# Two transformer layers in fp32: first norm tile by tile, another order of the first weights and products, and transposes tied behind the w1 matmuls

## Chip, core and metric

The kernel runs on one core of one Trainium2 chip. A core has TensorE (PE, matmuls), VectorE (DVE), ScalarE (ACT), GpSimd (POOL) and SyncE (SP), each with its own instruction queue that is worked in order; DMAs are issued from SP, ACT and POOL. PE writes into PSUM banks, the others work on SBUF. The metric is the device time of one execution in microseconds.

## The reference

Two blocks, attention (A) and an MLP with the mish activation (B), run twice in turn on x of 2048 rows by 512, with shared weights for both layers, all float32:

```python
def _A_ref(x, wqkv, wo):        # H = 32 heads of Dh = 16
    qkv = (x @ wqkv).reshape(B, S, 3, H, Dh) ...
    scores = jnp.einsum("bhqd,bhkd->bhqk", q, k) * (Dh ** -0.5)
    p = _softmax(scores, axis=-1)
    o = jnp.einsum("bhqk,bhkd->bhqd", p, v)
    return o.transpose(...).reshape(B, S, D) @ wo
def _B_ref(x, w1, b1, w2):      # F = 1792
    h = jnp.einsum("bsd,df->bsf", x, w1) + b1
    act = h * jnp.tanh(stable_softplus(h))
    return jnp.einsum("bsf,fd->bsd", act, w2)
x = x + _A_ref(_layernorm(x), wqkv, wo)
x = x + _B_ref(_layernorm(x), w1, b1, w2)
x = x + _A_ref(_layernorm(x), wqkv, wo)
x = x + _B_ref(_layernorm(x), w1, b1, w2)
```

## The kernel before

The 2048 rows are held as four chunks c of 512 rows, each chunk as four tiles of 128 rows. A float32 operand of a matmul is split into a rounded high part and the low part that is left; `mm3` (L174) makes of one product three matmuls per step k of 128 (high by high, high by low, low by high). High parts are written by ACT, low parts by DVE or POOL (`split_psum` L170, the inner `split` of `split_load` L132).

**The first stage (qkv of layer 0).** Chunk c is normed by `norm_parts` (L181): per tile `bn_stats` and `bn_aggr` on DVE (stq, mvq), variance plus epsilon on DVE (veq, L188), its power of -1/2 on POOL (rsq, L189), the scaling on DVE (xnq, L209), then transposes on PE through the bank pair tpq (L222), and the high and low part, thq on ACT and tlq on DVE, two tiles (a half of 256 columns) at a time. `norm_parts` is a generator; its parts are called from the loop of products in `qkv` at the places that the tables `within` (L729 on) give as (number of the product, step k). The products (m, c) follow the list `order`: m 0 to 3 are q, 4 to 7 are k, two m to one weight block of 256 columns. Products one to five are (0,0), (4,0), (1,0), (5,0) and (0,1), so the first two need chunk 0 and the weights sqkv0 and sqkv2, and the fifth is the first to need chunk 1. Each product's result is split into pt (ACT, then DVE) and stored by a DMA on ACT's queue (scr). Before the data are there, PE runs matmuls on zeros (`warm_up`, WARM).

**Values and maxima.** After q and k come the value products of chunks 0 to 2 (`v_parts`, parts of three or more matmuls, va), with the first row maxima of the scores mixed in by `some_max`: two pairs of matmuls into a bank pair each (pm, tag mx, two bank pairs), each reduced by DVE (mxv, L331). Then the attention loop starts with scores (sp, ss) and the value products of chunk 3 (vp), which use the bank pairs of tag mx.

**The MLP.** For the pairs (c, f), f from 0 to 13, `hid` makes h from the w1 block (three matmuls for each of four k), a chain on ACT, DVE and POOL makes the activation's high and low part, and `outp`, two f later, adds its w2 products into mo. Between them stand the last attention projections (wo) in c = 0, and the norms of later chunks: `spread` hangs the parts of a norm behind `hid` of given (c, f). Weights w1 and w2 are loaded by SP in the order of the program, each when a buffer of the pool blk comes free. Outside of the stages where PE's order is written out by hand (`att.pe`), the build orders the instructions of each engine by itself from program order and data, and may pull a transpose of a norm ahead of the matmuls that stand before it in the program.

Of the kernel before, what the change touches and what calls it, by code (L numbers as in the profile page):

```python
# [10 lines left out]
F32R = mybir.dt.float32r  # L11
BF16 = mybir.dt.bfloat16
AF = mybir.ActivationFunctionType
ALU = mybir.AluOpType
# [4 lines left out]
P = 128  # L19
S, D, H, DH, F = 2048, 512, 32, 16, 1792  # L20
NCH = 4
# [21 lines left out]
FILL = 12  # L43
KEEP = 2
PREP = 7
WARM = (4, 3)
GSTEPS = NCH * NKT
STEPS = NG * GSTEPS
HEADS = STEPS * HG
# [19 lines left out]
def kernel(ctx: ExitStack, tc: tile.TileContext, x, wqkv, wo, w1, b1, w2, out):  # L69
# [24 lines left out]
    def b8(shape, dt, name):  # L94
        return blk.tile(shape, dt, tag="blk", name=name)
# [21 lines left out]
    def behind(ins):  # L117
        return tc.keep_in_program_order(ins)
# [7 lines left out]
    def split_load(key, src, a, b, later, raw=None, low=nc.gpsimd):  # L126
        t = b8([P, 2, a, b], F32R, "s" + key)
        if raw is None:
            raw = tmp.tile([P, a, b], F32, tag="raw", name="r" + key, bufs=3)
        behind(nc.sync.dma_start(raw, src))  # L130

        def split():  # L132
            behind(nc.scalar.activation(t[:, 0], raw, AF.Copy))
            behind(low.tensor_tensor(t[:, 1], raw, t[:, 0].bitcast(F32), op=ALU.subtract))
            unkept.append((key, t))

        later.append(split)
        return t

    def split_keep(hooks, at, key, src, a, b):  # L140
# [40 lines left out]
    def norm_parts(src, nm, got, key, tag, fine=False, pin=lambda ins: ins, pe=lambda ins: ins, halves=False):  # L181
        st = tmp.tile([P, NCH, 6], F32, tag="st", name=f"st{nm}")
        mv = tmp.tile([P, NCH, 2], F32, tag="mv", name=f"mv{nm}")
        ve = tmp.tile([P, NCH], F32, tag="ve", name=f"ve{nm}")
        rs = tmp.tile([P, NCH], F32, tag="rs", name=f"rs{nm}")

        def rstd(t, n):
            pin(nc.vector.tensor_scalar(ve[:, t : t + n], mv[:, t : t + n, 1], EPS, None, op0=ALU.add))  # L188
            nc.gpsimd.tensor_tensor(rs[:, t : t + n], ve[:, t : t + n], mhalf[:, t : t + n], op=ALU.pow)  # L189

        for t in range(NCH):
            pin(nc.vector.bn_stats(st[:, t], src[:, t]))
            pin(nc.vector.bn_aggr(mv[:, t], st[:, t]))
            if fine:
                rstd(t, 1)
        if not fine:
            rstd(0, NCH)
        yield
        th = b8([P, KT, CW], F32R, f"th{nm}")
        tl = b8([P, KT, CW], F32R, f"tl{nm}")  # L200
        got[key] = (th, tl)

        def scaled(t, tag):
            if tag == "raw":
                xn = tmp.tile([P, 2, 512], F32, tag=tag, name=f"xn{nm}{t}", bufs=3)[:, 0]
            else:
                xn = t512(tag, f"xn{nm}{t}")
            pin(
                nc.vector.tensor_scalar(  # L209
                    xn, src[:, t], mv[:, t, 0:1], rs[:, t : t + 1], op0=ALU.subtract, op1=ALU.mult  # L210
                )
            )
            return xn

        if tag == "mx":
            xns = [scaled(t, ("f", "ah")[t // 2]) for t in range(NCH)]
            yield
            for u in range(NCH // 2):
                tp = ps.tile([P, 2, 512], F32, tag=tag, name=f"tp{nm}{u}")
                for e in range(2):  # L220
                    for k in range(KT):
                        pe(nc.tensor.transpose(tp[:, e, ts(k, P)], xns[2 * u + e][:, ts(k, P)], ident))  # L222
                two = ts(u, 2 * P)
                split_psum(
                    th[:, :, two].rearrange("p k (t n) -> p k t n", n=P),
                    tl[:, :, two].rearrange("p k (t n) -> p k t n", n=P),
                    tp.rearrange("p t (k n) -> p k t n", n=P),
                    pin,
                )
                yield  # L230
            return
        for t in range(NCH):
            xn = scaled(t, "raw" if tag == "acc" else "f")
            if halves:
                yield
            tp = pbank(tag, f"tp{nm}{t}")
            for k in range(KT):
                pe(nc.tensor.transpose(tp[:, ts(k, P)], xn[:, ts(k, P)], ident))
            split_psum(th[:, :, ts(t, P)], tl[:, :, ts(t, P)], tp.rearrange("p (k n) -> p k n", k=KT), pin)
            yield  # L240

    def spread(hooks, at, src, nm, got, key):
        parts = norm_parts(src, nm, got, key, "acc")
        for c, f in at:
            hooks.setdefault((c, f), []).append(lambda: next(parts, None))

# [211 lines left out]
    def load_qkv(l, wts, which, later, low=nc.gpsimd):  # L458
        raw = None
        for j in which:  # L460
            key = f"qkv{j}"
            if l:
                wts[j] = ready(key, l, True)
            elif j < 4:
                wts[j] = split_load(key, *cols(wqkv, j), later, low=low)
            else:
                if raw is None:
                    raw = b8([P, 2, 2, D], F32, "rawv")
                wts[j] = split_load(key, *rows2(wqkv[:, 2 * D : 3 * D], j - 4), later, raw[:, j - 4])
# [4 lines left out]
    def qkv(l, att, wts, tt, order, within, due):  # L474
        scr = att.scr
        ahead = [0]

        def some_max():
            if ahead[0] < AHEAD + PRE:
                for n in range(2):  # L480
                    att.max_mm(ahead[0], n)
                ahead[0] += 1

        done = 0
        spare = []
        parts = iter(())
        for n, (m, c) in enumerate(order):
            for fn in within.get((n, 0), []):
                fn()
            w = wts[m // 2]  # L490
            if n % 2:
                if not spare:
                    two = b8([P, 2, 2, CW], F32R, f"pt{l}{m}{c}")
                    spare += [two[:, 0], two[:, 1]]
                pt = spare.pop(0)
            else:
                pt = tmp.tile([P, 2, CW], F32R, tag="raw", name=f"pt{l}{m}{c}", bufs=3)
            th, tl = tt[c]
            acc = pbank("s", f"qk{l}{c}{m}")
            for k in range(KT):  # L500
                for fn in within.get((n, k), []) if k else []:
                    fn()
                mm3(
                    acc,
                    [(w[:, 0, k, ts(m % 2, P)], w[:, 1, k, ts(m % 2, P)], th[:, k], tl[:, k])],
                    first=k == 0,
                    last=k == KT - 1,
                    pe=att.pe,
                )
            split_psum(pt[:, 0], pt[:, 1], acc)  # L510
            nc.scalar.dma_start(
                scr[m][:, :, ts(c, CW)].bitcast(F32).rearrange("a p n -> p a n"), pt.bitcast(F32)
            )
            for fn in due.get((m, c), []):
                fn()
            for _ in range(2):
                next(parts, None)
            if m in (0, 4):
                done += 1
                if done == 2 * NCH:  # L520
                    parts = att.prep_qk(0)
                    for _ in range(2 * PREP):
                        next(parts)
            elif done == 2 * NCH and m in MAX_M:
                some_max()
        i = 0
        for c in range(NCH - 1):
            for _ in v_parts(l, c, wts, tt, att, False):
                i += 1
                if i % 3 == 0:  # L530
                    some_max()

    def v_parts(l, c, wts, tt, att, paired):
# [88 lines left out]
    def mlp(l, x2s, w1t, w2t, tts, dst, hooks):  # L622
        acts, obs = {}, {}

        def hid(c, f):
# [3 lines left out]
            mm3(  # L629
                acc,  # L630
                [(w[:, 0, k, ts(f % 2, P)], w[:, 1, k, ts(f % 2, P)], th[:, k, :], tl[:, k, :]) for k in range(KT)],
            )
            nm = f"{l}{c}{f}"
            hb, e, r = t512("f", "hb" + nm), t512("he", "he" + nm), t512("hr", "hr" + nm)
# [63 lines left out]
            keep(*unkept.pop(0))  # L698

    xc = [load_x(0)]  # L700
    load_qkv(0, wts, (0, 2), splits, nc.vector)
    xc += [load_x(c) for c in range(1, NCH)]
    nc.sync.dma_start(b1t, b1.rearrange("(f p) -> p f", p=P))
    att = attention(0)
    att.chained = True
    norms = [norm_parts(xc[c], f"q0{c}", tt, c, "mx", c == 0, behind, att.pe) for c in range(NCH)]
    warm = b8([P, CW], F32, "warm")
    nc.vector.memset(warm, 0.0)

# [3 lines left out]
            att.pe(nc.tensor.matmul(acc, warm[:, 0:P], warm, start=True, stop=True))  # L713

    warm_up(0, WARM[0])
    for i in range(4):
        next(norms[0])
        if i > 1:
            splits.pop(0)()
    warm_up(1, WARM[1])  # L720
    for l in range(2):
        due, within = {}, {}
        if l == 0:
# [2 lines left out]
            due[4, 2] = [lambda: load_qkv(0, wts, (4, 5), later)]  # L726
            due[0, 3] = [lambda: split_all(splits)]
            due[5, 2] = [lambda: split_all(later)]
            for c, (n0, n1, n2) in enumerate(((0, 0, 2), (2, 3, 5), (4, 6, 7)), 1):  # L729
                for at in ((n0, 0), (n1, 0), (n2, 1), (n2, 3)):  # L730
                    within.setdefault(at, []).append(lambda c=c: next(norms[c]))
        else:
            order = [(0, 0), (0, 1), (4, 0), (4, 1), (1, 0), (0, 2), (4, 2), (1, 1), (1, 2), (5, 0), (5, 1), (0, 3), (4, 3)]
# [126 lines left out]
```

## Time and profile before

| | |
|---|---|
| runs | 3551.27, 3558.86, 3556.11 us; median 3556.11 |
| profiled execution | 3554.46 us, span 3552.7 us |
| granted TensorE clock, mean | 0.999 |
| qkv and values, layer 0 | 0 to 168 us |
| attention loop, layer 0 | 168 to 1424 us |
| projections and MLP, layer 0 | 1424 to 1790 us |
| qkv and values, layer 1 | 1790 to 1934 us |
| attention loop, layer 1 | 1934 to 3189 us |
| projections and MLP, layer 1 | 3189 to 3553 us |

A row of the timeline has the start in us from the span's start, the us from its first start to its last end, the engine (ACTq and SPq are issues of DMAs; PEld are weight loads), the source line, the operation, what it writes <- reads, the shape, the number of instructions merged into the row, and in brackets the idle time of the engine before it with what ended it. Busy times of matmuls are modelled and overlap: the step from start to start tells PE's pace. A row of a table of windows has, after the window and its length, the busy us (and instructions) of PE, PEld, DVE, ACT and POOL, then the granted clock, the share of the DMA engines and GB/s.

### The profile page before, as it was taken

The numbers are of one execution on the slowest core, as the hardware profiler recorded it, in microseconds if no ns is written. First come the engines' busy times: TensorE is split into PE (matmuls) and PEld (weight loads), VectorE is DVE, ScalarE is ACT, GpSimd is POOL, SyncE is SP. The second block draws the span as 40 slices with busy tenths as digits, with TensorE's granted clock in tenths as the row PEclk, the third lists the DMA queues.
The fourth block names the chain that finished last, engine by engine and source line by source line (L and its number), as shares of the span: only waits on it lengthen the run. The fifth ranks groups of instructions, "written<-read, shape, count | busy, mean of one in ns | idle before, by whom it ended". The sixth has DMA issues, their size and how long they took to land.

```text
span 3552.7 us, 69170 instructions
## 1 busy us (share of the span) xinstructions
PE 3531.6 (99%) x28718; PEld 1938.4 (55%) x28718; DVE 2963.1 (83%) x3039; ACT 2520.7 (71%) x3401; POOL 521.6 (15%) x571
## 2 busy tenths in 40 slices
PE   9999999999999999999999999999999999999999
PEld 7644444444444444778876444444444444447887
DVE  5789999999999994756646999999999999947555
ACT  3188888888888888344522888888888888874444
POOL 2100100000000002444410000000000000024443
PEclk9999999999999999999999999999999999999999
DMA  7641312213132124510164211112111121245100
GB/s 250 218 99 47 83 44 76 59 52 71 44 80 46 45 80 70 159 60 13 59 221 140 53 37 39 38 29 44 32 35 38 41 35 41 68 78 161 50 13 24
DMA packets 139430, 255.11 MB, mean 72 GB/s; under 512 B 29348, under 2 KB 73316, under 8 KB 125292
## 3 DMA queue, kind: packets, MB, share of 16 engines
q1 hardware_dynamic: 112196, 174.04, 19.6%
q10 hardware_dynamic: 19176, 43.06, 3.4%
q0 software_dynamic: 7744, 33.60, 3.3%
q8 instruction: 225, 3.69, 0.5%
q14 instruction: 89, 0.73, 0.1%
HBM read 149.43 MB, written 100.14 MB: 70 GB/s over the span
## 4 chain that ended last, share of the span: by engine, by line
PE 95%; DMA 2%; DVE 1%; issue 1%; ACT 1%; POOL 1%; ACTq 0%; SPq 0%; DVEq 0%; POOLq 0%
PE pv L401 30%; PE pm L327 17%; PE ss L385 13%; PE sp L375 10%; PE mo L179 3%; PE mo L177 3%; PE mo L178 3%; PE h L179 3%; PE h L177 3%; PE h L178 3%; PE qk L177 1%; PE qk L178 1%; PE qk L179 1%; PE va L177 1%; PE wo L177 1%
## 5 line engine op out<-in xcount | busy, mean ns | idle before, releaser
L331 DVE TENSOR_REDUCE mxv<-pm 128x2 f32<-128x1024 f32 x2048 | 2385.6, 1218 | 135.5 <-PE pm L327 85.1
L376 ACT ACTIVATE p<-sp 128x1024 f32<-128x1024 f32 x1366 | 1395.9, 1022 | 19.3 <-PE sp L375 15.0
L401 PE MATMUL pv<-p,va 128*32 128x256 f32 (+2 forms) x16032 | 1166.9, 392 | 0.1
L327 PE MATMUL pm<-ks,qs 48*128 48x512 f32 x4096 | 1096.5, 446 | 0.3
L386 ACT ACTIVATE p<-ss 128x512 f32<-128x512 f32 x1364 | 814.5, 597 | 348.6 <-PE ss L385 263.1
L375 PE MATMUL sp<-qs,ks 50*128 50x512 f32 x2732 | 726.2, 447 | 0.3
L401 PEld LDWEIGHTS pv<-p,va 128*32 128x32 f32 x16032 | 367.7, 108 | 499.2 <-issue 421.5
L327 PEld LDWEIGHTS pm<-ks,qs 48*128 48x128 f32 x4096 | 450.0, 184 | 345.7 <-issue 210.0
L385 PE MATMUL ss<-qs,ks 50*128 50x512 f32 x1364 | 611.0, 448 | 0.0
L385 PEld LDWEIGHTS ss<-qs,ks 50*128 50x128 f32 x1364 | 252.0, 185 | 329.5 <-ACT p L386 222.8
L375 PEld LDWEIGHTS sp<-qs,ks 50*128 50x128 f32 x2732 | 261.3, 183 | 200.3 <-ACT p L376 119.1
L346 POOL CAST np<-nt 128x32 fp32r<-128x32 f32 x64 | 13.3, 208 | 2214.0 <-DVE nt L344 2214.0
L642 POOL TENSOR_TENSOR hb<-hb,he 128x512 f32<-128x512 f32 x110 | 149.2, 1356 | 190.3 <-DVE he L638 186.2
L645 POOL TENSOR_TENSOR hb<-hb,hr 128x512 f32<-128x512 f32 x110 | 150.5, 1368 | 139.5 <-DVE ah L644 134.7
L644 DVE TENSOR_TENSOR ah<-hb,hr 128x512 fp32r<-128x512 f32 x112 | 77.1, 689 | 111.5 <-ACT hr L640 67.2
L639 ACT ACTIVATE hr<-he 128x512 f32<-128x512 f32 x112 | 70.8, 632 | 125.0 <-DVE he L638 82.2
L635 ACT ACTIVATE hb<-h,b1t 128x512 f32<-128x512 f32 x112 | 77.0, 687 | 111.8 <-PE h L179 102.9
L637 ACT ACTIVATE he<-he 128x512 f32<-128x512 f32 x112 | 70.8, 632 | 103.0 <-DVE he L636 97.6
L171 ACT ACTIVATE pt<-qk 128x512 fp32r<-128x512 f32 x64 | 37.8, 597 | 148.4 <-PE qk L179 109.9
L636 DVE TENSOR_SCALAR he<-hb 128x512 f32<-128x512 f32 x112 | 70.8, 632 | 70.3 <-ACT hb L635 60.0
L646 DVE TENSOR_TENSOR al<-hb,ah 128x512 fp32r<-128x512 f32 x112 | 88.3, 789 | 32.5 <-POOL hb L645 32.3
L638 DVE SCALAR_TENSOR_TENSOR he<-he 128x512 f32<-128x512 f32 x112 | 79.7, 712 | 28.4 <-ACT he L637 27.5
(232 smaller groups left out, 3245.0 us busy)
## 6 DMA issues: line engine op xcount, KB each, us to landing
scr<-pt ACTq DMA_DIRECT2D x64, 512.0 KB
qs<-scr SPq DMA_DIRECT2D x174, 128.0 KB
ks<-scr SPq DMA_DIRECT2D x174, 128.0 KB
vscr<-v SPq DMA_DIRECT2D x32, 512.0 KB
va<-vscr SPq DMA_DIRECT2D x64, 256.0 KB
oscr<-ot SPq DMA_DIRECT2D x64, 256.0 KB
ww<-sw POOLq DMA_DIRECT2D x14, 1024.0 KB, 4.8
num<-oscr SPq DMA_DIRECT2D x64, 128.0 KB
```

Source lines behind the costliest of these rows:

```text
L177: pe(nc.tensor.matmul(acc, ah, bh, start=first and i == 0, stop=False))
L178: pe(nc.tensor.matmul(acc, ah, bl, start=False, stop=False))
L179: pe(nc.tensor.matmul(acc, al, bh, start=False, stop=last and i == n - 1))
L327: nc.tensor.matmul(pm[:, e], qs[u][rows, q0 : q0 + P], ks[u][rows, ts(n, 512)], start=True, stop=True)
L331: nc.vector.tensor_reduce(self.mxs[b][:, 2 * u : 2 * u + 2, qt, n], pm, axis=AX.X, op=ALU.max)
L375: self.pe(nc.tensor.matmul(sp[:, e], k, q, start=True, stop=True))
L376: nc.scalar.activation(self.pts[-1][:, 0:n], sp[:, 0:n], AF.Exp, scale=SCALE)
L385: self.pe(nc.tensor.matmul(sp, k, q, start=True, stop=True))
L386: nc.scalar.activation(self.pts[i // 3][:, 2], sp, AF.Exp, scale=SCALE)
L401: nc.tensor.matmul(self.accs[b][ts(h, VW), cols], self.va[b // NCH][:, kt, h, :], self.pts[j][:, e, cols], start=kt == 0 and q0 == 0, stop ...
L642: mul.tensor_tensor(hb, hb, e, op=ALU.mult)
L645: mul.tensor_tensor(hb, hb, r, op=ALU.mult)
```

## The change

- WARM is (4, 1, 1) in place of (4, 3); one matmul on zeros stands between the two halves' transposes of chunk 0, one behind them.
- `split` becomes two steps, `high` and `lowpart`, called apart. The first weight's high part is called before the first thq. The second weight's low part moves from DVE to POOL.
- The addition of epsilon moves from DVE to POOL, in all norms. The norms of the first stage are fine: each tile has its own addition and power, and each tile's scaling follows on DVE behind the next tile's statistics.
- The first two products of layer 0 are ordered by parts: high by high, low weight by high, high by low (the second with its last two exchanged), four matmuls each.
- The places of chunk 1 to 3's norm parts among the products move.
- `some_max` is called after value parts 1, 4, 7, ... in place of 3, 6, 9, ... in both layers.
- In both MLPs, transposes of a norm are tied to stand behind the last matmul of the `hid` that was issued before them.

```diff
-WARM = (4, 3)
+WARM = (4, 1, 1)
...
-        def split():
+        def high():
             behind(nc.scalar.activation(t[:, 0], raw, AF.Copy))
+
+        def lowpart():
             behind(low.tensor_tensor(t[:, 1], raw, t[:, 0].bitcast(F32), op=ALU.subtract))
             unkept.append((key, t))
-        later.append(split)
+        later += [high, lowpart]
...
         def rstd(t, n):
-            pin(nc.vector.tensor_scalar(ve[:, t : t + n], mv[:, t : t + n, 1], EPS, None, op0=ALU.add))
+            nc.gpsimd.tensor_scalar(ve[:, t : t + n], mv[:, t : t + n, 1], EPS, None, op0=ALU.add)
...
+        def next_scaled():
+            xns.append(scaled(len(xns), ("f", "ah")[len(xns) // 2]))
+
+        for t in range(NCH):
+            pin(nc.vector.bn_stats(st[:, t], src[:, t]))
+            pin(nc.vector.bn_aggr(mv[:, t], st[:, t]))
+            if fine:
+                rstd(t, 1)
+                if t and tag == "mx":
+                    next_scaled()
...
         if tag == "mx":
-            xns = [scaled(t, ("f", "ah")[t // 2]) for t in range(NCH)]
+            while len(xns) < NCH:
+                next_scaled()
...
+    hidden = []
+
+    def behind_hidden(ins):
+        tc.add_manual_dep(ins.ins, hidden[-1].ins.name, ..., reason="issue order")
...
-        parts = norm_parts(src, nm, got, key, "acc")
+        parts = norm_parts(src, nm, got, key, "acc", pe=behind_hidden)
...
-            for k in range(KT):
+            if l == 0 and n < 2:
+                for i, (part, t) in enumerate(((0, th), (0, tl), (1, th)) if n else ((0, th), (1, th), (0, tl))):
+                    for k in range(KT):
+                        start, stop = i == k == 0, i == 2 and k == KT - 1
+                        att.pe(nc.tensor.matmul(acc, w[:, part, k, ts(m % 2, P)], t[:, k], start=start, stop=stop))
+            for k in range(KT if l or n > 1 else 0):
...
-                if i % 3 == 0:
+                if i % 3 == 1:
                     some_max()
...
+                pe=lambda ins: hidden.__setitem__(slice(None), [ins]),
...
-    load_qkv(0, wts, (0, 2), splits, nc.vector)
+    load_qkv(0, wts, (0,), splits, nc.vector)
+    load_qkv(0, wts, (2,), splits)
...
-    norms = [norm_parts(xc[c], f"q0{c}", tt, c, "mx", c == 0, behind, att.pe) for c in range(NCH)]
+    norms = [norm_parts(xc[c], f"q0{c}", tt, c, "mx", True, behind, att.pe) for c in range(NCH)]
...
-    for i in range(4):
-        next(norms[0])
-        if i > 1:
-            splits.pop(0)()
+    next(norms[0])
+    splits.pop(0)()
+    next(norms[0])
+    next(norms[0])
     warm_up(1, WARM[1])
+    splits.pop(0)()
+    next(norms[0])
+    warm_up(2, WARM[2])
+    split_all(splits)
...
-            for c, (n0, n1, n2) in enumerate(((0, 0, 2), (2, 3, 5), (4, 6, 7)), 1):
-                for at in ((n0, 0), (n1, 0), (n2, 1), (n2, 3)):
+            for c, spots in enumerate((((0, 0), (0, 0), (2, 2), (3, 1)), ((2, 0), (2, 0), (5, 1), (5, 3)), ((4, 0), (4, 0), (7, 1), (7, 3))), 1):
+                for at in spots:
```

More of the change, by code (lines that the diff above doesn't have):

```diff
@@ L187, in rstd @@
         def rstd(t, n):
-            pin(nc.vector.tensor_scalar(ve[:, t : t + n], mv[:, t : t + n, 1], EPS, None, op0=ALU.add))
+            nc.gpsimd.tensor_scalar(ve[:, t : t + n], mv[:, t : t + n, 1], EPS, None, op0=ALU.add)
             nc.gpsimd.tensor_tensor(rs[:, t : t + n], ve[:, t : t + n], mhalf[:, t : t + n], op=ALU.pow)
[L191 to L201, printed above, removed]
+        xns = []
         def scaled(t, tag):
@@ L213, in scaled @@
             return xn
+        def next_scaled():
[7 more added lines that the diff above has]
+                    next_scaled()
+        if not fine:
+            rstd(0, NCH)
+        yield
+        th = b8([P, KT, CW], F32R, f"th{nm}")
+        tl = b8([P, KT, CW], F32R, f"tl{nm}")
+        got[key] = (th, tl)
         if tag == "mx":
-            xns = [scaled(t, ("f", "ah")[t // 2]) for t in range(NCH)]
+            while len(xns) < NCH:
+                next_scaled()
             yield
@@ L240, in norm_parts @@
             yield
+    hidden = []
+    def behind_hidden(ins):
+        tc.add_manual_dep(
+            ins.ins,
+            hidden[-1].ins.name,
+            mybir.DependencyInfo(mybir.DependencyClass.NoSync, mybir.DependencyReason.DATA),
+            reason="issue order",
+        )
     def spread(hooks, at, src, nm, got, key):
-        parts = norm_parts(src, nm, got, key, "acc")
+        parts = norm_parts(src, nm, got, key, "acc", pe=behind_hidden)
         for c, f in at:
```

## The prediction

> **What bounds the kernel now.** I read the page's first part, then the idle time of TensorE by what ended it, then the timeline of the first 31 us, of the places where a stage ends, and of the stop in the second half of the MLP.
>
> ```profile
> span 3552.7 us, 69170 instructions
> PE 3531.6 (99%) x28718; PEld 1938.4 (55%) x28718; DVE 2963.1 (83%) x3039; ACT 2520.7 (71%) x3401; POOL 521.6 (15%) x571
> ...
> PE tpq L222 <- DVE xnq L209: 3.6, 2, 1.8
> ...
> PE mo L177 <- DMA w24l<-ww: 2.0, 1, 2.0
> PE vp L177 <- DVE mxv L331: 0.9, 1, 0.9
> PE tpm L238 <- DVE x L617: 0.8, 1, 0.8
> ```
>
> TensorE (PE) is the bound: outside these few waits its matmuls follow each other without a stop. Each wait is us in all, times, longest; the MLP of layer 1 has the mo and the tpm row once more, with the same numbers. So the change can gain little beyond what stands in such rows, some 10 us, and it costs whatever new wait it puts in front of PE. The long attention loops keep their order on every engine and count as nothing.
>
> **The first norm and the first products.** The rows of today, in microseconds from the span's start:
>
> ```profile
> 4.66 0.56 POOL L189 TENSOR_TENSOR rsq<-veq,mhalf 128x1 f32<-128x1 f32 x1 [3.05 <-DVE veq L188]
> 8.16 0.87 POOL L189 TENSOR_TENSOR rsq<-veq,mhalf 128x1 f32<-128x1 f32 x1 [0.51 <-DVE veq L188]
> 8.00 1.91 DVE L209 TENSOR_SCALAR xnq<-x,mvq,rsq 128x512 f32<-128x512 f32 x4
> 9.74 1.02 ACT L171 ACTIVATE thq<-tpq 128x1024 fp32r<-128x1024 f32 x1 [7.72 <-PE tpq L222]
> 10.66 1.05 ACT L133 ACTIVATE sqkv<-rqkv 128x1024 fp32r<-128x1024 f32 x1
> 10.80 1.22 DVE L172 TENSOR_TENSOR tlq<-tpq,thq 128x1024 fp32r<-128x1024 f32 x1 [0.89 <-ACT thq L171]
> 11.94 1.22 DVE L134 TENSOR_TENSOR sqkv<-rqkv,sqkv 128x1024 fp32r<-128x1024 f32 x1
> 13.07 1.22 DVE L172 TENSOR_TENSOR tlq<-tpq,thq 128x1024 fp32r<-128x1024 f32 x1
> 16.06 0.18 DVE L193 BATCH_NORM_AGGREGATE mvq<-stq 128x2 f32<-128x6 f32 x1
> 16.16 0.66 DVE L192 BATCH_NORM_STATS2 stq<-x 128x6 f32<-128x512 f32 x1
> 17.80 0.69 DVE L172 TENSOR_TENSOR pt<-qk,pt 128x512 fp32r<-128x512 f32 x1 [0.19 <-ACT pt L171]
> 14.35 0.51 PE L178 MATMUL qk<-tlq,sqkv 128*128 128x512 f32 x1 [0.92 <-DVE tlq L172]
> 22.32 1.11 PE L222 MATMUL tpq<-ident,xnq 128*128 128x128 f32 x8 [1.78 <-DVE xnq L209]
> 28.95 0.39 PE L177 MATMUL qk<-thq,sqkv 128*128 128x512 f32 x1
> 29.18 0.39 PE L178 MATMUL qk<-tlq,sqkv 128*128 128x512 f32 x1
> 1.60:8.10 6.50, 5.21 (x8) 1.93 (x8) 4.00 (x13) 0.42 (x1) 1.69 (x4) 1.00 0.87 301
> ```
>
> Tile by tile, the fourth scaled tile of chunk 0 still ends near 9.9, where the four end now (8.00 + 1.91): it hangs on the fourth tile of x and its own chain. The new thing is on ScalarE (ACT), where the rounding of the first weight (1.05) now stands ahead of thq. It needs that weight landed: x and the weight are 1.57 MB, 5.2 us at 301 GB/s from 1.6, so not before 6.8, and not after 10.66, where it runs today without a wait. I take 8.2, nearer the lower end, because the bytes arrive there and a landing shows some time later. Then thq runs 9.2 to 10.2 and the first tlq starts at 10.25, 0.55 earlier than now; the weight's low part and the second tlq follow at today's steps (1.14, 1.13, 1.13), and VectorE (DVE) is free at 13.66. The second weight's low part, 1.13 on DVE today, goes to GpSimd (POOL) at 2.4 and ends near 15.2, before the last four products that need it.
>
> The first product, all of th first, then starts at 11.6 and ends at 14.75 (its tl part waits for the second tlq); the second ends at 17.5 after twelve steps of 0.23. Products three and four, with the 16 transposes of chunk 1 inside them (0.8 per eight), end at 24.8. Today the fifth begins at 28.95, so four microseconds have been gained here, the waits of 1.8 and 0.9 among them.
>
> On the queues little moves: SP keeps its order but for one load of va that goes ahead of two stores of v, and the load of the fourth weight now follows POOL's low part at 15.2, about as late as now.
>
> What is late next is the low part of chunk 1. The fifth product takes (th, tl, th) step by step, so its second matmul needs both halves of tl, and in the new program's order the first half stands on DVE behind chunk 2's statistics and scalings, and behind the fourth product's low part. From 13.66 DVE has ahead of it 9 statistics (0.70 with the aggregate's 0.10 beside it), 8 aggregates, 8 scalings (1.91 / 4), 4 low parts of products (0.69) and the other half of tl (1.14): 6.3 + 0.8 + 3.8 + 2.8 + 1.1 = 14.8, and some 0.5 of waits (0.3 for the first product's low part, the rest for POOL). The half starts at 28.95 and ends at 30.15. PE's second matmul of that product goes at 30.2 against 29.18 now: **+1.0**. With a weight landed at 6.8 the scaled tile at 9.9 holds instead (-0.3); landed at 10.66, +2.4. Later tl halves (chunks 2 and 3) have DVE time to spare by the same sum, about 0.4 at least.
>
> The first matmul goes at 25.6, when ACT has thq (its second half stands on ACT behind the issue of a scr store, which waits for DVE's third low part at 24.1), so PE stands still in one piece from about 26.0 to 30.2. What such a stop does to the clock the MLP shows:
>
> ```profile
> 1517.00 0.39 PE L179 MATMUL wo<-wo1l,ol 128*128 128x512 f32 x1
> 1518.17 0.66 PE L238 MATMUL tpm<-ident,xnm 128*128 128x128 f32 x4 [0.79 <-DVE x L617]
> 1520.87 0.80 PE L177 MATMUL mo<-w24l,ah 128*128 128x512 f32 x1 [2.05 <-DMA w24l<-ww]
> 1521.46 0.63 PE L178 MATMUL mo<-w24l,ah 128*128 128x512 f32 x1
> 1521.89 0.63 PE L179 MATMUL mo<-w24l,al 128*128 128x512 f32 x1
> 1516.06 0.32 SPq L161 DMA_DIRECT2D w24l<-ww  x1
> 1521.00:1523.00 2.00, 2.00 (x5) 1.63 (x6) 0.00 (x0) 0.00 (x0) 0.72 (x1) 0.50 1.02 430
> ```
>
> The granted clock (third number from the end) falls to 0.50, and matmuls step by 0.43 instead of 0.23; after a wait of 1.8 (22.32) it does not fall. Some seven matmuls at +0.2 make **+1.4** for the new stop, from 0 (clock kept) to 1.7. The Trainium skill (TensorE: Matmul & The Clock Gate, What's actually happening) has the clock fall after an idle window of about 3.4 us that runs free, and rise after one busy window; the trace agrees, and by the rule alone the sum would be +1.7 here.
>
> **The edge between w1 matmuls and transposes.** Today the first transposes of chunk 2 (tpm) are pulled far ahead, into the stop above: PE ends its work at 1517.2, runs them, and then waits for w24, whose DMA left at 1516.06, when a wo weight's buffer came free. With the edge they stand after the w1 products of the next chunk's seventh column (in layer 1 the same), where PE has no wait. The stop stays as long, since w24 is issued by the same matmul and lands 4.8 later, and the transposes are paid:
>
> ```profile
> 1580.25 0.39 PE L179 MATMUL h<-thm,w13l 128*128 128x512 f32 x1
> 1580.48 0.60 PE L238 MATMUL tpm<-ident,xnm 128*128 128x128 f32 x4
> 1580.84 0.48 PE L177 MATMUL mo<-w22l,ah 128*128 128x512 f32 x1
> 1581.15 0.39 PE L178 MATMUL mo<-w22l,ah 128*128 128x512 f32 x1
> ```
>
> From 1580.25 to 1581.15 is 0.90, and two steps of 0.23 without them: 0.44, twice, **+0.9**. Queued behind the edge on PE are only that chunk's own mo matmuls; tl of chunk 2 is needed a whole chunk later. The stop is now 3.6 idle in one piece instead of 0.8 and 2.05; both layers are throttled today, so I add nothing (from -1.5, should a throttled stretch now fall into the wait, to +1). Moving the addition of epsilon from DVE to POOL hides in the MLP behind POOL's 15%.
>
> **Another phase of the maxima.** In the value products a pair of maxima (pm, two DVE reductions) stood after parts 3, 6, 9 and so on; it now stands after 1, 4, 7. The number of pairs is the same.
>
> ```profile
> 120.79 1.23 DVE L331 TENSOR_REDUCE mxv<-pm 128x2 f32<-128x1024 f32 x1 [0.66 <-PE pm L327]
> 122.53 3.56 DVE L331 TENSOR_REDUCE mxv<-pm 128x2 f32<-128x1024 f32 x3
> 123.18 1.11 PE L327 MATMUL pm<-ks,qs 48*128 48x512 f32 x4
> 124.22 0.50 PE L177 MATMUL va<-sqkv,thq 128*128 128x512 f32 x1
> ...
> 168.32 0.57 PE L375 MATMUL sp<-qs,ks 50*128 50x512 f32 x2
> 169.38 0.50 PE L177 MATMUL vp<-sqkv,thq 128*128 128x512 f32 x1 [0.50 <-DVE mxv L331]
> 1934.91 0.50 PE L177 MATMUL vp<-qkv4l,thq 128*128 128x512 f32 x1 [0.86 <-DVE mxv L331]
> ```
>
> The first pair's second half needs the bank that DVE's reduction of 122.53 frees at 123.76; that is why the four pm take 1.11. Standing six matmuls earlier, it waits for the same 123.76, and the six (6 x 0.23 = 1.37) come after it: +1.4 in each layer. At the other end the vp product no longer waits for the last reduction: -0.50 - 0.86. Net 2.75 - 1.36: **+1.4** (0 if DVE runs ahead by then).
>
> Sum: 1.0 + 1.4 + 0.9 + 1.4 = **+4.7**, on the profiled execution's 3554.46 (its span 3552.7 and 1.8 around it) 3559.2. The median shown, 3556.11, lies 1.65 above that execution and would go to 3560.8. I say 3560.
>
> **Rivals.** *Faster: the head start is kept.* If DVE gets to tl of chunk 1 by 24.8 (ACT or the landing earlier than worked out, or DVE steps shorter when not queued), the first stretch is worth -4.1 instead of +2.4, and the total is -1.8: 3554.3 on the median. Against it speaks that 14.8 of DVE work stands between 13.66 and that half whatever PE does.
>
> *Slower: POOL becomes the bound of the norm.* Every tile's scaling now waits for two steps in a row on POOL, addition and power, and DVE stands behind it. No row shows the addition: a power of 0.56 is the upper bound, nothing the lower, and I took 0.3. The power took 0.87 where it ran beside the scalings, and 0.56 alone. With 0.56 and 0.87 a tile takes 1.43 on POOL, 0.57 above my 0.86, and of the eight tiles ahead of the late half I count five without slack: 5 x 0.57 = +2.9 and a total of +7.6: 3563.7. It decides from an addition of about 0.5. For it speaks the row of 0.87; against it, that two tiles' statistics stand between most scalings. The Trainium skill (SBUF — State Buffer, SBUF: two separate sides) says DVE and POOL share a port pair under an exclusive lock that some DVE operations take whole; the row of 0.87 agrees. By it alone each POOL step beside a scaling could lose a whole one, 0.48 by the row of 1.91.
>
> *The waits only change places.* PE's stops at 68 to 78 us hang on DMAs that the products start; if these were the true bound, the first 2.4 would vanish into them, and the total is +2.3: 3558.4. Against: these stops are only 1.2 in all.
>
> **How the numbers follow.** The forecast has 0.5, POOL 0.2, the changed places 0.15, the kept head start 0.15. Executions shown lie within 3551.27 and 3558.86, so 0.2% (7.1) is about what can be told from no change. All but POOL's case and the forecast's upper tail (clock at 1.7, landing late) lie within it: slower 0.25; faster than 7.1 needs more than the waits in reach, 0.06; same 0.69. The range 3554 to 3568 runs from the kept head start to POOL's case with the scatter of the executions.
>
> **What would show it.** Right: PE idle before the second matmul of the fifth product, released by DVE's tlq, 4 us long, and a granted clock near 0.5 behind it; no idle before vp, but over 1 us inside the first pm pair of the value products; tpm of chunk 2 after its seventh w1 column, and a stop of 3.6 before mo with w24. Wrong: a fifth product before 28 us, or a gap in the attention loops.

## The result and the profile after

The changed kernel takes 3565.78 us (median of 9 runs, 3564.14 to 3569.55) beside 3556.11 for the kernel before in the same runs: a ratio of 1.0028 with a 95% interval of 1.0018 to 1.0038. It is slower, by 9.7 us, twice what the forecast's sum said. The profiled execution took 3565.78, its span is 3564.0 where it was 3552.7: 11.3 us to be explained.

The first part of the changed kernel's page:

```profile
span 3564.0 us, 69179 instructions
...
PE 3536.5 (99%) x28716; PEld 1943.1 (55%) x28716; DVE 2966.7 (83%) x3016; ACT 2521.5 (71%) x3401; POOL 537.3 (15%) x612
```

PE is still the bound, and it is busy for 4.9 us *more* although it has hardly a matmul more or less to run. That is not waiting; it is the same work done slower. The rest is waits, in the view of TensorE's idle time by what ended it (us in all, times, longest):

```profile
PE mo L179 <- DMA w24l<-ww: 6.9, 2, 3.5
PE qk L180 <- DVE tlq L174: 3.7, 1, 3.7
PE pm L346 <- DVE mxv L350: 3.3, 5, 1.2
PE qk L179 <- DVE pt L174: 2.5, 3, 1.4
```

Against the rows of before: the two waits of 1.8 for the scaled tiles (tpq) and those for the last maxima before vp are gone; a wait of 3.7 for tl, one for the maxima (pm) and a longer one for w24 have come. The same instruction's start in the two timelines tells where the 11.3 us arise (the losses are taken before rounding):

| stretch of PE, up to | before | after | lost here | forecast |
|---|---|---|---|---|
| last transposes of the first norm | 42.62 | 44.58 | 1.96 | 2.4 |
| first va product, layer 0 | 120.91 | 124.08 | 1.21 | 0 |
| first vp product (maxima), layer 0 | 169.38 | 173.42 | 0.86 | 0.87 |
| last sp of the attention, layer 0 | 1417.22 | 1420.99 | -0.26 | 0 |
| last mo, layer 0 (MLP) | 1789.62 | 1795.99 | 2.60 | 0.44 |
| first va product, layer 1 | 1886.42 | 1893.88 | 1.09 | 0 |
| first vp product (maxima), layer 1 | 1934.91 | 1944.74 | 2.37 | 0.51 |
| last sp, layer 1 | 3182.69 | 3192.21 | -0.30 | 0 |
| last mo, layer 1 (MLP) | 3547.20 | 3558.52 | 1.79 | 0.44 |

**The first norm** went as drawn, in the changed kernel's timeline (start, length, idle time in front and what ended it):

```profile
13.40 0.69 DVE L211 BATCH_NORM_STATS2 stq<-x 128x6 f32<-128x512 f32 x1
...
24.34 0.39 PE L181 MATMUL qk<-thq,sqkv 128*128 128x512 f32 x1
25.20 0.49 PE L179 MATMUL qk<-thq,sqkv 128*128 128x512 f32 x1 [0.47 <-ACT thq L173]
...
28.15 1.22 DVE L174 TENSOR_TENSOR tlq<-tpq,thq 128x1024 fp32r<-128x1024 f32 x1
29.43 0.63 PE L180 MATMUL qk<-tlq,sqkv 128*128 128x512 f32 x1 [3.73 <-DVE tlq L174]
```

Product four ends at 24.6, four microseconds ahead of before, and then the second matmul of product five stands until 29.43 for a half of tl that DVE reaches at 28.15.

**The maxima**, on PE, layer 0 and layer 1:

```profile
125.24 0.50 PE L346 MATMUL pm<-ks,qs 48*128 48x512 f32 x2 [0.19 <-DVE mxv L350]
126.97 0.51 PE L346 MATMUL pm<-ks,qs 48*128 48x512 f32 x2 [1.23 <-DVE mxv L350]
...
1896.77 0.79 PE L346 MATMUL pm<-ks,qs 48*128 48x512 f32 x2 [1.23 <-DVE mxv L350]
1897.49 0.79 PE L179 MATMUL va<-qkv4l,thq 128*128 128x512 f32 x1
```

The wait inside the first pair is the same 1.23 in both layers. Behind it the matmuls take 0.50 in layer 0 and 0.79 in layer 1: there the clock has fallen.

**The stop before w24**, layer 0, on PE:

```profile
1521.83 0.39 PE L181 MATMUL wo<-wo1l,ol 128*128 128x512 f32 x1
1525.76 0.80 PE L179 MATMUL mo<-w24l,ah 128*128 128x512 f32 x1 [3.55 <-DMA w24l<-ww]
```

Nothing stands between the last wo and the first product with w24, where the transposes of chunk 2 were: one stop of 3.55 instead of two.

**The clock.** Asked in stretches of 3.41 us that begin where it falls, the windows view of PE gives (stretch, its length, PE busy us, granted clock, DMA share and GB/s):

```profile
26.23:29.64 3.41, 0.21 (x1) 1.00 0.97 359
29.64:33.06 3.42, 3.42 (x9) 0.50 0.57 222
...
1521.27:1524.68 3.41, 0.94 (x5) 1.00 0.83 274
1524.68:1528.10 3.42, 2.34 (x6) 0.50 1.01 419
1528.10:1531.51 3.41, 3.41 (x10) 0.50 1.02 430
1531.51:1534.92 3.41, 3.41 (x16) 1.00 0.25 106
...
1893.32:1896.74 3.42, 2.03 (x9) 1.00 0.33 129
1896.74:1900.15 3.41, 3.38 (x8) 0.50 0.33 127
...
3296.20:3299.62 3.42, 2.42 (x6) 0.50 0.94 378
3299.62:3303.03 3.41, 3.41 (x10) 0.50 1.01 404
```

and of the kernel before, which has two slow stretches up to its last product:

```profile
1520.34:1523.75 3.41, 2.88 (x7) 0.50 1.02 423
...
3288.45:3291.86 3.41, 3.41 (x9) 0.50 1.02 408
```

At half clock half of the busy time is lost: (2.88 + 3.41) / 2 = 3.1 us before, (3.42 + 2.34 + 3.41 + 3.38 + 2.42 + 3.41) / 2 = 9.2 us after. So 6.1 of the 11.3 us are clock. The forecast had 1.4.

### The profile page after: what moved, and what is told of

It reads as the page before. It is cut to its first block, busy times and chain, and to the rows that moved or that the text cites. A ratio compares the mean times of both kernels' runs of the same rounds, so it can differ in the third digit from the quotient of the medians.

```text
span 3564.0 us, 69179 instructions
## 1 busy us (share of the span) xinstructions
PE 3536.5 (99%) x28716; PEld 1943.1 (55%) x28716; DVE 2966.7 (83%) x3016; ACT 2521.5 (71%) x3401; POOL 537.3 (15%) x612
## 4 chain that ended last, share of the span: by engine, by line
PE 95%; DVE 2%; DMA 1%; ACT 1%; POOL 1%; issue 0%; ACTq 0%; DVEq 0%; POOLq 0%
PE pv L420 30%; PE pm L346 17%; PE ss L404 13%; PE sp L394 10%; PE mo L181 3%; PE mo L179 3%; PE mo L180 3%; PE h L181 3%; PE h L179 3%; PE h L180 3%; PE qk L179 1%; PE qk L180 1%; PE qk L181 1%; PE wo L179 1%; PE va L179 1%; DMA scr<-pt 1%
## 5 line engine op out<-in xcount | busy, mean ns | idle before, releaser
L661 DVE TENSOR_SCALAR he<-hb 128x512 f32<-128x512 f32 x112 | 79.7, 712 | 62.6 <-ACT hb L660 50.0
L174 DVE TENSOR_TENSOR pt<-qk,pt 128x512 fp32r<-128x512 f32 x64 | 43.6, 686 | 69.5 <-ACT pt L173 66.9
```

## The experiments

Ten kernels, each with its own profile, timed in runs shared with the kernel before. A ratio is known to about 0.1%, 3.4 us, which does not part versions that lie 2 us from each other; where a verdict is finer, it rests on the same stretch in several traces.

**Three parts undone, one at a time.** First the maxima back after parts 3, 6, 9:

```
-                if i % 3 == 1:
+                if i % 3 == 0:
```

> The changed kernel with the maxima of the value products back after parts 3, 6, 9 in both layers. Theory: the first pair's wait (1.86 us in two places) shrinks to 0.4, the wait before the first vp (0.5 to 0.9) comes back, and in layer 1 the slow clock behind that wait (8 matmuls at +0.2) goes away: -0.9 in layer 0 and -2.4 in layer 1, so 3.3 less than the changed kernel, 3562.5. Rival 1, the forecast's own working (the clock is not touched): 0.9 and 0.5, 1.4 less, 3564.4. Rival 2, the wait for DVE only comes back at vp in full: no difference, 3565.8.

Second, no edge:

```
-        parts = norm_parts(src, nm, got, key, "acc", pe=behind_hidden)
+        parts = norm_parts(src, nm, got, key, "acc")
```

> The changed kernel without the edge from w1 matmuls to transposes. Theory: the first transposes of chunk 2 go back into the stop before the w24 product, so 0.44 a layer is saved, and the stop, cut in two, ends before the clock has fallen or shortly after: about 7 slow matmuls instead of 14, another 1.4 a layer. Together 3.6 less, 3562.2. Rival 1, the forecast's working (only the transposes): 0.9 less, 3564.9. Rival 2 (whether one or two stretches of low clock follow is chance from one execution to the next): between 0.9 and 3.6 less, and the low clock's length differs between the two layers of one trace.

Third, the kernel before with the edge and the new phase alone:

```
-        parts = norm_parts(src, nm, got, key, "acc")
+        parts = norm_parts(src, nm, got, key, "acc", pe=behind_hidden)
...
-                if i % 3 == 0:
+                if i % 3 == 1:
...
+                pe=lambda ins: hidden.__setitem__(slice(None), [ins]),
```

> The first norm, the first weights and the first products as before; edge and new phase of the maxima stay. Theory: the stop of 4 us before the second matmul of the fifth product and the slow clock behind it go, but the waits of 1.8, 0.9 and 1.8 come back, 2.0 less at the last transpose of the norm; the stop at 77 us, which grew by 1.2, shrinks with it: 3.2 less, 3562.6. Rival: the stop at 77 us hangs on the ScalarE queue's transfers and not on the first products, so it stays: 2.0 less, 3563.8. The waits at 1846 and 1861 us of layer 1 (1.1 more than before) stay in either case, if they come from the changed kernel's code, and go if they are scatter of the transfers.

Fourth, PE kept busy in the stop, with products of oh into a bank that nobody reads, tied between the last wo matmul and the first product with w24:

```
...
+                for _ in range(14):
+                    pe(nc.tensor.matmul(idle, oh[:, 0, 0:P], oh[:, 0], start=True, stop=True))
...
```

> The changed kernel with 14 matmuls of 512 columns, whose result nobody reads, between the last wo matmul and the first product with w24, in both layers. Theory: the clock falls because PE stands still, so it stays at 1.00 here, and the 13 or 14 matmuls that step by 0.43 behind the stop step by 0.23: 2.8 a layer, 5.6 less than the changed kernel, 3560.2; the stop itself keeps its end, since w24 lands when it lands. Rival: the matmuls behind the stop are slow because the weights stream in at 420 GB/s beside them, whatever PE did before: no gain, 3565.8, or 0.3 more where the filling runs past the landing.

Measured: medians (the first two rows repeat the runs of the result; the four new kernels stand against 3556.32 for the kernel before in their own runs), and in each trace the distance between the starts of two named instructions, and how many stretches ran at half clock:

| kernel | median | ratio (95%) | first va to first vp, layer 0 / 1 | last wo to last mo, layer 0 / 1 | slow: norm, maxima, w24 |
|---|---|---|---|---|---|
| before | 3556.11 | 1 | 48.47 / 48.49 | 272.62 / 263.62 | 0, 0, 1+1 |
| after | 3565.78 | 1.0028 (1.0018 to 1.0038) | 49.34 / 50.86 | 274.17 / 265.09 | 1, 0+1, 2+2 |
| maxima back | 3562.65 | 1.0019 (1.0010 to 1.0027) | 48.49 / 48.49 | 273.12 / 263.97 | 2, 0+0, 1+1 |
| no edge | 3564.13 | 1.0023 (1.0014 to 1.0033) | 50.88 / 49.34 | 272.35 / 263.39 | 2, 1+0, 1+1 |
| norm back | 3562.45 | 1.0018 (1.0010 to 1.0027) | 50.17 / 50.90 | 273.10 / 264.24 | 0, 0+1, 1+1 |
| filled stop | 3562.45 | 1.0020 (1.0011 to 1.0029) | 49.34 / 49.42 | 272.10 / 263.12 | 2, 0+0, 0+0 |

*Maxima back*: 3.1 below the changed kernel, as the theory said (3.3) and not the forecast's 1.4. In the old phase the stretch is 48.5 in every trace. In the new one it is 49.3 to 49.4 where the clock held (50.2 once, with a wait of 0.69 for ScalarE that no other trace has), and about 50.9 where it fell; the layer in which it fell is not the same from trace to trace. So 0.85 is the wait, right as forecast, and some 1.55 the clock, in about half of the cases.

*No edge*: 1.7 below, inside the 0.9 to 3.6 of rival 2. The table settles what the median can't: with the edge and one slow stretch the MLP's part takes 0.3 to 0.6 more than before (maxima back, norm back), which is the forecast's price of the transposes, 0.44; with the edge and two slow stretches it takes 1.5 more (after). One or two is therefore no property of the edge: all three kernels have the same stop of 3.4 to 3.6. It is where the stop falls, as the windows of the kernel with the maxima back show beside those of the changed kernel above:

```profile
1523.92:1527.33 3.41, 0.73 (x3) 1.00 1.01 411
1527.33:1530.74 3.41, 3.41 (x10) 0.50 1.01 425
1530.74:1534.16 3.42, 3.42 (x16) 1.00 0.78 328
```

There the stop ends inside the stretch that holds most of it, and the next is busy throughout; in the changed kernel the stop's end reaches 1.1 us into the next, PE is busy for 2.34 of it, and the clock stays down for one more. The rival of chance was right, and my theory (the edge itself doubles the slow stretch) was not: the trace of *norm in another order*, below, has two slow stretches there in layer 0 and one in layer 1.

*Norm back*: 3.3 below (theory 3.2). But the theory's second half, that the stop at 77 us goes with it, fell: this trace has waits of 1.0 and 0.4 there, the kernel before 0.4 and 0.2. And the 1.1 us lost in layer 1's q and k products can be scatter: the stretch from the last transposes to the first va of layer 1, which no kernel here alters, took 72.84 to 76.15 us in twelve traces, 72.85 in that of before and 73.93 in that of after. Undone one at a time, the three parts give 3.1, 1.7 and 3.3, together 8.1 of the 9.7 us.

*Filled stop*: 3.3 below, where the theory said 5.6 and the rival 0. Its trace keeps the clock at 1.00 before and behind w24 in both layers (its only slow stretches are in the first norm). The first two rows are layer 0; in the third, layer 1, the products with w24 run at full clock beside 438 GB/s, more than beside any slow stretch above, so the rival is out:

```profile
1522.59:1526.00 3.41, 2.63 (x12) 1.00 0.99 327
1526.00:1529.41 3.41, 3.41 (x16) 1.00 0.90 341
...
3300.00:3302.00 2.00, 2.00 (x11) 1.00 1.05 438
```

The missing 2.3 us have two causes that I can name but did not size apart: the theory counted two slow stretches a layer, as in the one trace it was made from, where 1 to 2 are usual; and the filling started 0.8 late and ran past the landing, which is due 4.9 after the issue at 1521.71 (the distance of the changed kernel: 1525.76 - 1520.89):

```profile
1523.83 3.52 PE L698 MATMUL idle<-oh 128*128 128x512 f32 x14 [0.78 <-DVE x L649]
1527.18 0.40 PE L179 MATMUL mo<-w24l,ah 128*128 128x512 f32 x1
```

**Taking the causes away.** If DVE's order is what loses the head start, another order keeps it; if a wo buffer holds up w24, freeing it earlier ends the stop. The places (product, step) of chunks 2 and 3 in the first norm:

```
-((2, 0), (2, 0), (5, 1), (5, 3)), ((4, 0), (4, 0), (7, 1), (7, 3))
+((3, 2), (3, 2), (5, 1), (5, 3)), ((5, 0), (5, 0), (7, 1), (7, 3))
```

> The changed kernel with the statistics and scalings of chunk 2 issued in the middle of the fourth product instead of the third, and those of chunk 3 in front of the sixth product, so that VectorE reaches both low halves of chunk 1 before them. Theory: the 4.0 us in front of the second matmul of the fifth product were this queue on VectorE alone, so they go, and the one or two stretches of 3.41 us at half clock behind them (1.7 us each) go too: 5.7 to 7.4 less than the changed kernel's 3565.8, 3559.2. Rival: the next limit takes it back (chunk 2's transposes late by as much, or the stops at 70 to 78 us, which hang on the ScalarE queue's transfers): 2 less, 3563.8.

The twelfth w1 column of chunk 0 tied behind the last wo matmul:

```
...
+                if (c, f) == (0, 11):
+                    tie(ins, last_wo[0])
...
```

> The changed kernel with its last 12 wo matmuls in front of the twelfth w1 column of chunk 0 instead of behind it (both layers), so that the wo0 buffer comes free, and w24's transfer starts, 12 x 0.228 = 2.7 us earlier. Theory: the stop of 3.5 us before the first product with w24 shrinks to 0.8 to 1.0, which is too short to lower the clock: 2.7 us and the 1 or 2 stretches at half clock (1.7 each) a layer, 8.8 to 12.2 less than the changed kernel, 3555.3. Rival: w24 does not wait for that buffer but for the queue in front of it, so its transfer starts when it did: 0, 3565.8.

*All together* is both of these, the maxima back and no edge; the fourth kernel is the one before with the second edit and nothing else.

> The changed kernel with the maxima back after parts 3, 6, 9, without the edge, with chunk 2's norm later as in e5_norm_order and the last wo matmuls earlier as in e6_wo_first. Theory: what the parts cost adds up, so the gains add up: 3.1 (measured for the maxima), 6.4 at the start, 10.2 at w24 and 0.9 for the transposes that go back into what is left of the stop, 20.6 less than the changed kernel: 3545.2, 11 less than before. Rival: the start's gain is taken back by the stops at 70 to 78 us: 3549.5.

> The kernel before with nothing but its last 12 wo matmuls in front of the twelfth w1 column of chunk 0 (both layers). Theory: its stop of 0.8 + 2.05 us there goes, all but some 0.2, and one stretch at half clock a layer with it: 2 x (2.7 + 1.7) = 8.8 less than before, 3547.5. Rival: as in e6_wo_first, the transfer starts when it did: 3556.3. Beside e7_best it tells what the first norm in its mended order is worth by itself: equal if that norm gives nothing, e7_best lower by 2 to 4 if its head start is kept.

| kernel | median (before 3556.20) | ratio (95%) | start of first va, layer 0, against before | first to last mo, layer 0 / 1 | slow stretches up to the last mo |
|---|---|---|---|---|---|
| before | | 1 | 0 | 326.14 / 318.23 | 2 |
| after | | | +3.2 | 328.39 / 319.67 | 6 |
| norm in another order | 3568.09 | 1.0035 (1.0022 to 1.0047) | +6.5 | 328.47 / 319.03 | 6 |
| wo first | 3556.15 | 1.0000 (0.9991 to 1.0009) | +0.9 | 323.12 / 314.44 | 4 |
| all together | 3552.90 | 0.9995 (0.9986 to 1.0004) | +4.4 | 322.70 / 313.75 | 1 |
| before, wo first | 3548.78 | 0.9979 (0.9971 to 0.9988) | +1.5 | 322.02 / 314.56 | 0 |

*Wo first* did what the theory said (3555.3): 9.6 below the changed kernel. The timeline has the transfer on the load queue, and PE, first of the changed kernel,

```profile
1520.89 0.32 SPq L163 DMA_DIRECT2D w24l<-ww  x1
```

then with wo first:

```profile
1517.38 0.32 SPq L163 DMA_DIRECT2D w24l<-ww  x1
...
1518.33 0.39 PE L181 MATMUL wo<-wo1l,ol 128*128 128x512 f32 x1
...
1522.26 0.50 PE L179 MATMUL mo<-w24l,ah 128*128 128x512 f32 x1 [0.82 <-DMA w24l<-ww]
```

In both, the transfer leaves while the last six wo matmuls run, and PE starts with w24 4.9 later; now twelve w1 matmuls lie between, 0.82 is left of the stop, and the clock stays up. On the kernel before the same edit gives 7.4 (theory 8.8), and no slow stretch is left in its trace: **this kernel, 3548.78, is faster than both.**

*Norm in another order* failed in both readings: it came out 2.3 above the changed kernel, too little to call it slower, where the theory had 6.6 less. The 4.0 us did go (0.9 was left), but chunk 2's transposes waited for their scaled tiles, 1.3 at the longest, and chunk 3's statistics, which I had put in front of the sixth product, now stood ahead of chunk 2's tl:

```profile
41.63 0.79 PE L180 MATMUL qk<-tlq,sqkv 128*128 128x512 f32 x1 [3.23 <-DVE tlq L174]
```

The same happened in *all together*, which came out at 3552.9 where theory and rival had 3545.2 and 3549.5: the gains at w24 and at the maxima add up, the one at the start does not exist in this order.

**Does the head start pay at all?** Two more orders on top of *all together*:

```
-((3, 2), (3, 2), (5, 1), (5, 3)), ((5, 0), (5, 0), (7, 1), (7, 3))
+((3, 2), (3, 2), (6, 1), (6, 3)), ((7, 0), (7, 0), (8, 1), (8, 3))
```

> e7_best with the rest of the first norm later still: chunk 2's transposes in the seventh product, chunk 3's statistics and scalings in front of the eighth, its transposes in the ninth, so that VectorE has each chunk's low halves ahead of the next chunk's statistics. e7_best still lost 1.0, 1.3, 0.7 and 3.4 us to VectorE at 26 to 42 us, and one stretch at half clock. Theory (only the order on VectorE costs there): the 3.4 us and the 1.7 us of clock go, about 1 each comes new at the eighth and the tenth product, where VectorE has just finished: 3 less than e7_best, 3550. Rival (VectorE is short of time in the first 45 us in any order, so each stop that is removed comes back at the next chunk): as e7_best, 3552.9 or above.

```
+((3, 2), (3, 2), (6, 1), (6, 3)), ((7, 0), (7, 0), (9, 1), (9, 3))
...
-            order = [(0, 0), (4, 0), (1, 0), (5, 0), (0, 1), (4, 1), (1, 1), (0, 2), (4, 2), (0, 3), (4, 3)]
+            order = [(0, 0), (4, 0), (1, 0), (5, 0), (0, 1), (4, 1), (1, 1), (5, 1), (0, 2), (4, 2), (1, 2), (0, 3), (4, 3)]
```

> e9_norm_late with one more product of chunk 1 in front of the first of chunk 2, and one more of chunk 2 in front of the first of chunk 3, 2.75 us of matmuls each, so that VectorE has that much more time. Theory: the waits of about 1 us for chunk 2's and chunk 3's low halves go, and the first norm at last keeps its head start of 4 us: 5 to 6 less than e7_best, 3547, and below e8_before_wo's 3548.8 by 2. Rival 1: the first q and k columns are all ready two products (5.5 us) later, and the stops at 70 to 80 us take that back: 3550 or above. Rival 2, as in e9_norm_late: 3552.9.

The first: 3550.76, ratio 0.9985 (0.9976 to 0.9994), nearer to its theory (3550) than to its rival (3552.9), though 2.1 us hardly part the two; its trace has no slow stretch and no stop longer than 1.0 in the first norm. The second: 3549.38, 0.9980 (0.9971 to 0.9989), no better than the kernel before with wo first. Here the head start is kept at last: the 281st matmul or transpose of these products starts at 68.63, where before has it at 70.99. Then ScalarE's queue stops, and PE behind it:

```profile
70.72 0.57 ACTq L543 DMA_DIRECT2D scr<-pt  x1
74.14 0.31 ACTq L317 DMA_DIRECT2D qs<-scr  x1
74.49 0.66 ACTq L310 DMA_DIRECT2D ks<-minus  x1
75.20 0.60 ACT L173 ACTIVATE pt<-qk 128x512 fp32r<-128x512 f32 x1 [8.38 <-PE qk L181]
```

```profile
76.58 0.50 PE L179 MATMUL qk<-thq,sqkv 128*128 128x512 f32 x1 [2.35 <-DVE pt L174]
```

The load of qs goes out 3.4 us behind the store in front of it; the rounding of a finished product queues behind that load on ScalarE, its low part behind the rounding on DVE, and PE waits for the bank. One slow stretch follows. Rival 1 named this, with a time (3550 or above) that the measurement does not part from 3549.4. That the load waits for a store's landing is read from the order of the rows and was not tested. Nor need the head start be what makes the stop: the kernel before with wo first has no head start, and waits for 0.3, 1.0 and 0.3 us at 69 to 79 us.

## Why the prediction was right and where it was wrong

The time lies in the range (3554 to 3568), on the slow side. The likeliest case, 3560 and no difference that can be told, did not come; the case of slower by over 0.2%, at 0.25, did. That the range holds the time is in part luck: its upper end was drawn for POOL's case, which did not come, and the sum, +4.7, is half of what was measured. Point by point:

- *The first norm up to product four*: right throughout. The weight's rounding starts at 7.99 (I took 8.2), the first product at 11.60 (11.6), product four ends at 24.6 (24.8).
- *tl of chunk 1 late behind DVE's queue, +1.0*: right in mechanism, and 0.8 too dear. I had 14.8 us of work and 0.5 of waits between 13.66 and 28.95; the trace has 14.75 in all, from 13.40 to 28.15. So PE goes at 29.43, +0.25.
- *The slow clock behind it, +1.4 (0 to 1.7)*: 1.7 in this trace, but five traces with this norm have one or two slow stretches there, so its upper end should have been 3.4. By the rule of the Trainium skill that I set beside the row (TensorE: Matmul & The Clock Gate, What's actually happening) it was 1.7, with which this trace agrees; three of the five stay down for a second stretch.
- *The edge, 0.44 a layer and no clock*: the transposes' price was right (0.3 to 0.6 with one slow stretch). "Both layers are throttled today, so I add nothing" is the step that failed: the stop, one piece now, can throttle twice, and did in both layers. I had +1 as the upper end; each layer lost 1.5 from the last wo on. (Layer 0's 2.60 are these 1.54, the 0.35 of the next point, and 0.71 between the first mo and the last wo, where PE waits for al with w23 in another order of h and mo matmuls, which I had not priced. The 0.71 is not the edge's: it stands in the kernel without the edge, and not in norm back, which has the edge.)
- *Epsilon on POOL, nothing in the MLP*: almost. In the changed kernel's timeline DVE has two statistics of the next tiles ahead of the MLP's first scaled tile, which the kernel before (first two rows) scales first, and the first transposes wait:

```profile
1431.95 0.54 DVE L209 TENSOR_SCALAR xnm<-x,mvm,rsm 128x512 f32<-128x512 f32 x1
1432.40 1.28 DVE L192 BATCH_NORM_STATS2 stm<-x 128x6 f32<-128x512 f32 x2
...
1435.85 1.29 DVE L211 BATCH_NORM_STATS2 stm<-x 128x6 f32<-128x512 f32 x2
1437.05 0.53 DVE L201 TENSOR_SCALAR xnm<-x,mvm,rsm 128x512 f32<-128x512 f32 x1
...
1437.64 0.55 PE L247 MATMUL tpm<-ident,xnm 128*128 128x128 f32 x3 [0.37 <-DVE xnm L201]
```

  It is 0.35 a layer up to the first mo. No run moved the addition alone, but the traces divide by it: the stretch from the last sp to the first mo takes 46.26 to 46.28 us in the three kernels with the addition on DVE (before, norm back, before with wo first) and 46.56 to 46.63 in the nine with it on POOL, in both layers.
- *The maxima, +1.4 net*: 0.86 measured in layer 0 where 1.37 - 0.50 was written, to within a hundredth; in layer 1, 2.37 where 0.51 was. The wait was the same; the clock behind it was not in my sum at all, since it holds after a wait of 1.8 in the row of 22.32. That row was one case, and the maxima's waits, 1.4 us of idle time in all, lower it in six places of twelve.
- *Waits at 70 to 78 us and in layer 1's products*: no term in my sum, 2.3 in this pair of traces. In layer 1 it can be scatter of transfers, the profile of before happening to be at the low end of twelve; in layer 0 its cause stays open.

So the waits were placed and sized nearly right, and the clock was under-counted: 1.4 where the profiled executions differ by 6.1. Of the rivals, POOL as the bound is out: an addition takes 0.22 to 0.48 in the timeline, and DVE waited 0.37 for POOL between 13.4 and 28.15. "The waits only change places" was named against small evidence, 1.2 us of stops; the one trace of the last experiment shows it for a head start that is kept.

## What to carry to other kernels

Price a stop of PE as the stop plus 1.7 us for each 3.41 us stretch that it may slow, and look at several traces before calling that number a property of the code. When a weight lands late, look for the matmul that frees its buffer, and move that matmul forward: a reordering of twelve matmuls in each layer was worth 7 us here, more than everything else tried. When an operation is moved earlier on an engine with one queue, list what is now behind it for each later consumer, to the last chunk: each order that cured one chunk's wait handed it to the next until the products were given time as well.

## What the runs showed of the hardware that was not expected

The clock falls and rises only at the edges of a fixed grid of 3.413 us, to within 0.01 us in each of the twelve traces: in the changed kernel's trace the slow stretches begin 438, 109 and 410 times that length after one another. In the twelve traces laid on this grid, after the first 25 us (in which 0.49 and 0.51 once each passed without a fall), each stretch at full clock in which PE was busy for at most 0.58 was followed by a slow one, each with 0.63 or more was not, and between them both occurred; a slow stretch with a busy share of at most 0.78 was followed by another, with 0.83 or more it was the last. So the maxima's two waits, 0.19 and 1.23 us, slow the clock or not by where they fall. In the changed kernel's layer 0 an edge of the grid, at 125.22, cuts off the first, and the stretch holds 1.25 us of idle time; in the kernel without the edge of transposes one stretch holds both, 1.43 us:

```profile
125.22:128.63 3.41, 2.16 (x9) 1.00 0.57 158
128.63:132.04 3.41, 3.41 (x16) 1.00 0.60 214
```

```profile
123.90:127.32 3.42, 1.99 (x11) 1.00 0.49 112
127.32:130.73 3.41, 3.41 (x9) 0.50 0.78 279
```

Six of the twelve such places in the six kernels with the new phase were slowed. The Trainium skill (TensorE: Matmul & The Clock Gate, Why this matters for your kernels) advises against idle gaps above some 3 us; these rows show that shorter ones can be enough.
